# Dilated attention into a SiLU MLP on one core: transposes and products of a kind in one clump each, loads of later batches issued in the second layer

## The chip, the core and the metric

The kernel runs on one core of a Trainium2 chip. The metric is device time in microseconds (us) of one execution; less is better. Times of several executions are given as their median with the lowest and highest. A core has five engines with instruction queues of their own that run side by side and wait for each other by semaphores: TensorE (PE in the profile: matmuls, with PEld for its weight loads), VectorE (DVE), ScalarE (ACT), GpSimd (POOL, here almost only the issue of loads) and SyncE (SP, the issue of stores). Each engine takes its own instructions in order.

## The reference

Inputs are q, k and v of 8 batches, 8 heads, 576 positions and 64 channels, and two matrices, w_in (512x2048) and w_out (2048x512).

```python
scores = q @ k.T / 8                     # per batch and head, 576 x 576
rel = row - column
mask = (rel >= 0) & (rel < 32)                              # heads 0 to 3, "plain"
mask = (rel >= 0) & (rel < 128) & (rel % 4 == 0)            # heads 4 to 7, "dilated"
attn = softmax of the scores inside the mask
x = (attn @ v), heads side by side       # 4608 tokens of 512
h = x @ w_in
out = (h * sigmoid(h)) @ w_out           # 4608 x 512, float32
```

Every row looks at 32 positions: of a plain head the last 32, of a dilated head every fourth one of the last 128.

## The kernel before, in words

**Two kinds, blocks of 32 rows.** A batch has two kinds of heads, z=0 (the four plain ones) and z=1 (the four dilated ones). A dilated head is split into 4 residue classes of positions, in each of which it is a plain band. Rows go in blocks of 32 (QB); a block needs 64 keys (KB). So the attention is made of many matmuls that use only a part of TensorE's 128x128 array: 64x64 or 64x32 of it, as the shapes in the profile say. The kernel orders them so that neighbours lie in different quarters of the array.

**The stages of one kind of one batch**, each a function:

- load_qk (L91) and load_v (L124) issue the loads on GpSimd's queue, shift_v (L143) moves rows of v inside the chip. The tiles n0 and n1 (q and k, two buffers each) and vw (v, one for even and one for odd batches) are written.
- transpose (L244): which=1 is k, which=0 is q. 36 small transposes (z=0) or 24 (z=1) on TensorE into two PSUM tiles, which VectorE copies out for one half and ScalarE for the other (L264, L273).
- scores (L392): 72 or 80 small matmuls into three PSUM tiles; VectorE scales and masks them (L414, L423) and takes the row maximum (L430).
- exps (L445): on ScalarE, one exponential of 128x64 for each of 8 or 10 blocks (L458), for hi=0 and hi=1, the two heads of a pair.
- normal (L463): on VectorE, the reciprocal of the row sum and its product with the exponentials, pn (L471 to L474).
- turn and turned (L478, L487): 4 or 5 full-array transposes of pn on TensorE (L483), copied out by VectorE (L491).
- values (L493): the products with v, 32 small matmuls for each of two *phases* (L519) and 4 or 8 more for the last 64 rows (last_values, L565 and L576). A PSUM tile belongs to one pair of heads, n. In phase 0 the even blocks of n=0 and the odd blocks of n=1 are done, in phase 1 the others, so that the two row halves of the array never write the same bank at one time.
- finish (L589): after each phase VectorE copies the halves just made into xT (L598, and L585 or L587 for the last rows).

**The MLP.** layer1 (L602) multiplies xT of one batch by one of 16 column tiles f of w_in: 8 full-array matmuls (L607) into a PSUM tile h of the pool big, then Silu on ScalarE (L615). layer2 (L635) makes 4 (even batches) or 5 (odd ones) output tiles of 128 tokens, 16 matmuls each (L643), copied out by VectorE (L651) and stored by SyncE's queue (L653). Batch 0 has its first layer in two parts (L619).

**PSUM.** It has 8 banks. The pool big has 2 buffers of two banks, shared by h and o; the pool ps has 4 buffers of one bank for all else.

**The order by hand.** The order of the instructions is the order in which the program issues them (a manual schedule). Each batch has a plan (plan_of, L676) that hangs attention work of the next batches between its matmuls. A plan has *steps*: step f (0 to 15) is just ahead of the column tile f of the first layer, step 16 + 4x + y just ahead of the y-th four matmuls of output tile x. at(s, fn, ...) appends a call to step s. The helpers transposes (L659) and later (L663) spread the work of one kind over steps; later's six steps are: normal of hi=0, turn of hi=0, normal of hi=1, turn of hi=1, products of phase 0, products of phase 1. For batches b from 2 on (L732 to L749) the plan holds, in the first layer, the transposes of z=1 and the whole later part of z=0 of batch b+1, then the scores of z=1; in the second layer the transposes and scores of z=0 of batch b+2 and the later part of z=1 of batch b+1.

A step only fixes the place in each engine's queue. An instruction starts when its engine reaches it and the semaphores that it waits for are set. The table of ScalarE's functions (Exp or Silu) has to be changed twice a batch (ACT_TABLE_LOAD); the build puts such a load ahead of the first activation that needs it. A copy needs none.

The plan is called from layer2's loop (L642) and from the outer loop (L801):

```python
                if f % 4 == 0:
                    plan(NFF + 4 * x + f // 4)
...
            for f in range(NFF):
                plan(f)
                layer1(b, f)
        layer2(b, plan)
```

Of the kernel before, what the change touches and what calls it, by code (L numbers as in the profile page):

```python
# [14 lines left out]
P = 128  # L15
W = 32
DIL = 4
# [10 lines left out]
def kernel(  # L28
# [461 lines left out]
        pt = a["pt", z, hi] = ptp.tile([P, WM // 2, P], F16, tag="pt", name=f"ptT_{b}_{z}_{hi}")  # L490
        nc.vector.tensor_copy(pt[:, 0:n], a["ptT", z, hi][:, 0:n])  # L491

    def values(b, z, phase):  # L493

        a = att(b)
        if phase == 0:
            a["x", z] = [
                ps.tile([P, NS], F32, tag="ps", name=f"x_{b}_{2 * z + n}") for n in (0, 1)
            ]
            a["xs", z] = ps.tile([P, 2, KB], F32, tag="ps", name=f"xs_{b}_{z}")  # L500

        for i in range(8):
            for n in (0, 1):
                e = (n + phase) % 2
                r = slice(e * KB, e * KB + KB)
                for hi in (0, 1):
                    x = a["x", z][n][hi * D : hi * D + D]
                    pt = a["pt", z, hi]
                    if z == 0:
                        j = 2 * i + e  # L510
                        w = plain_v(a, j, 2 * n + hi)
                        dst = x[:, j * QB : (j + 1) * QB]
                        p = pt[r, 2 * n + j // 8, i % 4 * QB : i % 4 * QB + QB]
                    else:
                        j, c = i // 4 * 2 + e, i % 4
                        w = class_v(a, j, 2 * n + hi, c)
                        dst = x.rearrange("d (i r) -> d r i", r=DIL)[:, c, j * QB : (j + 1) * QB]
                        p = pt[r, 2 * n + j // 2, c * QB : c * QB + QB]
                    nc.tensor.matmul(dst, w, p, start=True, stop=True)  # L519
        last_values(b, z, phase)  # L520

    def values0(z, part):


        a = att(0)
        x = a["x", z] = [
            ps.tile([P, 2, SA], F32, tag="ps", name=f"x_0_{z}_{part}_{e}") for e in (0, 1)
        ]
        pt = a["pt", z, part]
        for i in range(4):  # L530
            for n in (0, 1):
                for e in (0, 1):
                    for hi in (0, 1):
                        dst = x[e][hi * D : hi * D + D, n]
                        if z == 0:
                            j = 8 * part + 2 * i + e
                            w = plain_v(a, j, 2 * n + hi)
                            dst = dst[:, (2 * i + e) * QB : (2 * i + e + 1) * QB]
                        else:
                            w = class_v(a, 2 * part + e, 2 * n + hi, i)  # L540
                            dst = dst.rearrange("d (i r) -> d r i", r=DIL)[:, i, e * QB : e * QB + QB]
                        nc.tensor.matmul(
                            dst, w, pt[e * KB : e * KB + KB, 2 * hi + n, i * QB : i * QB + QB],
                            start=True, stop=True,
                        )
        if part:
            a["xs", z] = ps.tile([P, 2, KB], F32, tag="ps", name=f"xs_0_{z}")
            last_values(0, z, 0)

    def finish0(z, part, copy=nc.vector.tensor_copy):  # L550
# [5 lines left out]
        if part:  # L556
            last_finish(0, z, 0, copy)

    def last_values(b, z, phase):
        a = att(b)  # L560
        r = slice(phase * KB, phase * KB + KB)
        for hi in (0, 1):
            if z == 0:
                for n in (0, 1):
                    nc.tensor.matmul(  # L565
                        a["xs", z][hi * D : hi * D + D, n, phase * QB : (phase + 1) * QB],
                        plain_v(a, 16 + phase, 2 * n + hi),
                        a["pt", z, 1][r, 4, (2 * n + hi) * QB : (2 * n + hi + 1) * QB],
                        start=True, stop=True,
                    )  # L570
            else:
                x = a["xs", z][hi * D : hi * D + D, phase].rearrange("d (i r) -> d r i", r=DIL)
                for c in range(DIL):
                    o = (2 * hi + c % 2) * QB
                    pt = a["pt", z, 1][r, 4 + c // 2] if b == 0 else a["pt", z, c // 2][r, 4]
                    nc.tensor.matmul(  # L576
                        x[:, c, :], class_v(a, 4, 2 * phase + hi, c), pt[:, o : o + TL],
                        start=True, stop=True,
                    )

    def last_finish(b, z, phase, copy=nc.vector.tensor_copy):
        xT, xs = att(b)["xT"], att(b)["xs", z]
        if z == 0:
            o = phase * QB
            copy(xT[:, 0:2, NS + o : NS + o + QB], xs[:, :, o : o + QB])  # L585
        else:
            copy(xT[:, 2 + phase, NS:S], xs[:, phase])  # L587

    def finish(b, z, phase, copy=nc.vector.tensor_copy):  # L589


        a = att(b)
        xT = a["xT"]
        run = QB * (DIL if z else 1)
        for n in (0, 1):
            e = (n + phase) % 2
            f = lambda y: y.rearrange("d (m e c) -> d m e c", e=2, c=run)[:, :, e, :]
            copy(f(xT[:, 2 * z + n, 0:NS]), f(a["x", z][n]))  # L598
        last_finish(b, z, phase, copy)


    def layer1(b, f):  # L602
# [53 lines left out]

    both = (nc.vector.tensor_copy, nc.scalar.copy)

    def transposes(at, b, z, steps):  # L659
        for n in (0, 1):  # L660
            at(steps[n], transpose, b, z, 1 - n, both)

    def later(at, b, z, steps):  # L663

        at(steps[0], normal, b, z, 0)
        at(steps[1], turn, b, z, 0)
        at(steps[1], turned, b, z, 0)
        at(steps[2], normal, b, z, 1)
        at(steps[3], turn, b, z, 1)
        at(steps[3], turned, b, z, 1)  # L670
        at(steps[4], values, b, z, 0)
        at(steps[4], finish, b, z, 0)
        at(steps[5], values, b, z, 1)
        at(steps[5], finish, b, z, 1)

    def plan_of(b):  # L676
        ev = {}
# [8 lines left out]
        if b == 0:  # L686

            at(-15, normal, 0, 1, 1)
            at(-14, turn, 0, 1, 1)
            at(-14, turned, 0, 1, 1)  # L690
            at(-13, normal, 0, 0, 1)
            at(-12, values0, 1, 1)
            at(-12, finish0, 1, 1)
            at(-10, turn, 0, 0, 1)
            at(-10, turned, 0, 0, 1)
            at(-8, last_values, 0, 1, 1)
            at(-8, last_finish, 0, 1, 1)
            at(-7, values0, 0, 1)
            at(-7, finish0, 0, 1)
            at(-3, last_values, 0, 0, 1)  # L700
            at(-3, last_finish, 0, 0, 1)
            transposes(at, 1, 0, (1, 3))
            at(5, scores, 1, 0)
            transposes(at, 1, 1, (7, 9))
            at(10, load_qk, 3)
            at(10, load_v, 2)
            at(10, shift_v, 2, nc.gpsimd, (ALL,))
            at(12, scores, 1, 1)
            for hi in (0, 1):
                at(12, shift, 1, 1, hi)  # L710
            at(14, shift_v, 1, nc.sync, (ALL,))
            all_exps(1, 0)
            all_exps(1, 1)
            later(at, 1, 0, (20, 22, 23, 25, 26, 27))
            later(at, 1, 1, (25, 27, 27, 29, 30, 31))
        elif b == 1:
            at(0, load_v, 3)
            at(0, shift_v, 3, nc.gpsimd, (ALL,))
            transposes(at, 2, 0, (2, 4))
            transposes(at, 2, 1, (8, 10))  # L720
            transposes(at, 3, 0, (14, 15))
            at(6, scores, 2, 0)
            at(11, load_qk, 4)
            at(12, scores, 2, 1)
            all_exps(2, 0)
            all_exps(2, 1)
            at(17, scores, 3, 0)
            at(18, exps, 3, 0, 0)
            at(18, exps, 3, 0, 1)
            later(at, 2, 0, (22, 24, 25, 27, 28, 29))  # L730
            later(at, 2, 1, (29, 31, 32, 34, 35, 36))
        else:  # L732
            if b + 2 < B:
                at(0, load_v, b + 2)
                at(0, shift_v, b + 2, nc.gpsimd, (ALL,))
            if b + 1 < B:
                transposes(at, b + 1, 1, (2, 6))
                later(at, b + 1, 0, (0, 2, 2, 4, 7, 8))
                if b + 3 < B:
                    at(8, load_qk, b + 3)  # L740
            if b + 2 < B:
                transposes(at, b + 2, 0, (12, 14))
                at(17, scores, b + 2, 0)
                at(18, exps, b + 2, 0, 0)
                at(18, exps, b + 2, 0, 1)
            if b + 1 < B:
                at(10, scores, b + 1, 1)
                all_exps(b + 1, 1)
                later(at, b + 1, 1, (22, 24, 25, 27, 28, 29))  # L749

        def plan(s):
            for fn, args in ev.pop(s, ()):
# [84 lines left out]
```

## Time and profile before

| what | us |
|---|---|
| three runs: median (lowest to highest) | 348.04 (346.62 to 348.13) |
| the profiled execution | 348.62 |
| its span, first to last instruction | 346.8 |
| TensorE busy | 321.5 (93%) |
| ScalarE busy | 216.4 (62%) |
| VectorE busy | 184.6 (53%) |
| GpSimd busy | 88.3 (25%) |

The profile is that of one execution. "Busy" of TensorE counts matmuls from start to modelled end, and they overlap; distances between the starts of neighbouring groups say more. A line of a timeline reads: start, busy time, engine, line of the program, operation, written tile <- read tiles, shape, count, and in brackets idle time ahead of it and what ended it. In rows of stretches PEclk is the clock granted to TensorE, 1.00 being full. The costliest groups are the second layer's matmuls (L643, 132.2), the first layer's (L607, 119.1), the exponentials (L458, 94.2) and Silu (L615, 72.8).

### The profile page before, as it was taken

The numbers are of one execution on the slowest core, as the hardware profiler recorded it, in microseconds if no ns is written. First come the engines' busy times: TensorE is split into PE (matmuls) and PEld (weight loads), VectorE is DVE, ScalarE is ACT, GpSimd is POOL, SyncE is SP. The second block draws the span as 40 slices with busy tenths as digits, with TensorE's granted clock in tenths as the row PEclk, the third lists the DMA queues.
The fourth block names the chain that finished last, engine by engine and source line by source line (L and its number), as shares of the span: only waits on it lengthen the run. The fifth ranks groups of instructions, "written<-read, shape, count | busy, mean of one in ns | idle before, by whom it ended". The sixth has DMA issues, their size and how long they took to land.

```text
span 346.8 us, 11988 instructions
## 1 busy us (share of the span) xinstructions
PE 321.5 (93%) x5216; PEld 203.4 (59%) x5216; DVE 184.6 (53%) x410; ACT 216.4 (62%) x746; POOL 88.3 (25%) x148
## 2 busy tenths in 40 slices
PE   4549899889999999999999999999999999999995
PEld 4437654447754577557765577557755577457642
DVE  7766337765657756555656356555656353440021
ACT  2693547506699756995589365995589356916400
POOL 8726656333400254024400560023000000000000
PEclk9999989999999999999999999999999999999999
DMA  6999999939802199029901964039002100110022
GB/s 81 164 219 208 205 200 219 187 75 136 132 10 93 60 131 144 33 66 144 150 8 66 174 110 75 33 81 145 4 2 92 62 4 2 60 50 14 0 79 76
DMA packets 45062, 32.90 MB, mean 95 GB/s; under 512 B 21872, under 2 KB 39536, under 8 KB 45008
## 3 DMA queue, kind: packets, MB, share of 16 engines
q0 software_dynamic: 38816, 21.74, 45.8%
q1 hardware_dynamic: 6192, 10.39, 8.5%
q8 instruction: 41, 0.67, 0.8%
q14 instruction: 13, 0.11, 0.1%
HBM read 37.75 MB, written 9.44 MB: 136 GB/s over the span
## 4 chain that ended last, share of the span: by engine, by line
PE 76%; DVE 8%; DMA 6%; ACT 5%; issue 2%; POOL 1%; SPq 0%; POOLq 0%
PE h L607 30%; PE o L643 27%; PE h L626 6%; ACT pe L458 4%; PE t L260 3%; PE x L519 3%; DVE pn L474 3%; PE pt L483 2%; DMA vw<-in_v_dram 2%; DMA vw<-vw 2%; DMA n<-in_k_dram 2%; ACT L458 1%; PE s L318 1%; DVE kC L273 1%; PE s L306 1%
## 5 line engine op out<-in xcount | busy, mean ns | idle before, releaser
L643 PE MATMUL o<-w_out,gT 128*128 128x512 f16 x576 | 132.2, 379 | 0.0
L615 ACT ACTIVATE gT<-h 128x576 f16<-128x576 f32 x112 | 72.8, 650 | 84.0 <-PE h L607 84.0
L607 PE MATMUL h<-xT,w_in 128*128 128x288 f16 x896 | 119.1, 286 | 0.0
L607 PEld LDWEIGHTS <-w_in 128*128 128x128 f16 x896 | 84.2, 98 | 22.6 <-issue 0.2
L458 ACT ACTIVATE pe<-ms,nm 128x64 f32<-128x64 f32 x284 | 94.2, 333 | 3.3 <-DVE nm L387 3.2
L643 PEld LDWEIGHTS <-gT 128*128 128x128 f16 x576 | 53.8, 98 | 58.0
L651 DVE COPY ob<-o 128x512 f32<-128x512 f32 x36 | 24.8, 690 | 59.1 <-PE o L643 59.1
L458 ACT ACTIVATION_READ_ACCUMULATOR pe<-ms,nm 128x1 f32 x284 | 53.0, 187 | 0.0
L414 DVE SCALAR_TENSOR_TENSOR ms<-s,mask 128x512 f32<-128x512 f32 x28 | 19.2, 687 | 33.1 <-PE ss L306 15.3
L127 POOL DMA_DIRECT2D vw<-in_v_dram x16 | 10.0, 632 | 98.1 <-PE xs L576 98.1
L598 DVE CAST xT<-x 128x256 f16<-128x256 f32 x56 | 21.1, 418 | 11.5 <-PE xs L565 7.4
L474 DVE TENSOR_TENSOR pn<-pe,r 128x640 f16<-128x640 f32 (+2 forms) x32 | 25.3, 792 | 1.1
L430 DVE TENSOR_REDUCE nm<-ms 128x10 f32<-128x640 f32 (+1 forms) x28 | 22.0, 787 | 1.0
L626 PE MATMUL h<-xT,w_in 128*128 128x256 f16 (+1 forms) x128 | 20.6, 317 | 0.8 <-DVE xT L555 0.8
L491 DVE COPY ptT<-pt 128x640 f16<-128x640 f16 (+2 forms) x32 | 15.0, 470 | 11.4 <-PE pt L483 11.4
L633 ACT ACTIVATE gT<-h 128x512 f16<-128x512 f32 (+1 forms) x16 | 10.4, 650 | 16.3 <-PE h L626 16.3
L102 POOL DMA_DIRECT2D n<-in_q_dram x28 | 16.3, 592 | 15.5 <-DMA w_in<-in_moe_w_in_dram 5.5
L483 PE MATMUL pt<-ident,pn 128*128 128x128 f16 x152 | 14.7, 229 | 5.6 <-DVE pn L474 5.2
L102 POOL DMA_DIRECT2D n<-in_k_dram x28 | 16.3, 591 | 10.4 <-DMA w_in<-in_moe_w_in_dram 3.6
L483 PEld LDWEIGHTS <-pn 128*128 128x128 f16 x152 | 10.0, 101 | 13.7 <-DVE pn L474 11.1
L519 PEld LDWEIGHTS <-vw 64*64 64x64 f16 x896 | 9.8, 108 | 10.9 <-issue 10.9
L626 PEld LDWEIGHTS <-w_in 128*128 128x128 f16 x128 | 12.9, 107 | 5.1 <-issue 0.8
(79 smaller groups left out, 260.2 us busy)
## 6 DMA issues: line engine op xcount, KB each, us to landing
out_dram<-ob SPq DMA_DIRECT2D x36, 256.0 KB, 2.0
n<-in_k_dram POOLq DMA_DIRECT2D x28, 144.0 KB, 5.3
n<-in_q_dram POOLq DMA_DIRECT2D x28, 144.0 KB, 5.3
vw<-in_v_dram POOLq DMA_DIRECT2D x8, 288.0 KB, 6.1
vw<-in_v_dram POOLq DMA_DIRECT2D x16, 128.0 KB, 3.3
w_in<-in_moe_w_in_dram POOLq DMA_DIRECT2D x4, 512.0 KB, 10.7
w_out<-in_moe_w_out_dram POOLq DMA_DIRECT2D x4, 512.0 KB, 10.6
vw<-vw POOLq DMA_DIRECT2D x12, 128.0 KB, 3.8
```

Of the source, the lines that this page charges most:

```text
L102: nc.gpsimd.dma_start(out=qk[b, z, which][i * HF : i * HF + UPS[z]].rearrange("p h u d -> p h (u d)"), in_=src[b, h : h + 2].rearrange("h ...
L430: nc.vector.tensor_reduce(out=nm[:, 0:w], in_=ms[:, 0:w], axis=AX.X, op=ALU.max, negate=True)
L458: nc.scalar.activation(pe[:, t, :], ms[:, t, :], AF.Exp, bias=nm[:, t : t + 1], accum_out=l[:, t : t + 1],)
L474: nc.vector.tensor_tensor(pn[:, 0:w], a["pe", z, hi][:, 0:w], r[:, 0:w, None].broadcast_to([P, w, KB]), ALU.mult)
L483: nc.tensor.transpose(t[:, i, :], a["pn", z, hi][:, 2 * i : 2 * i + 2].rearrange("p t c -> p (t c)"), ident)
L519: nc.tensor.matmul(dst, w, p, start=True, stop=True)
L598: copy(f(xT[:, 2 * z + n, 0:NS]), f(a["x", z][n]))
L607: nc.tensor.matmul(h[:, half, 0:HS], w_in16[:, c, f * P : f * P + P], xT[:, c, half * HS : half * HS + HS], start=(c == 0), stop=(c == MC ...
L615: nc.scalar.activation(gT[:, f, s0 : s0 + S].rearrange("p (a c) -> p a c", a=2), h[:, :, 0:HS], AF.Silu)
L626: nc.tensor.matmul(h[:, i, 0 : c1 - c0], w_in16[:, c, (f + i) * P : (f + i + 1) * P], xT[:, c, c0:c1], start=(c == 0), stop=(c == MC - 1),)
L643: nc.tensor.matmul(o, gT[:, f, t * P : (t + 1) * P], w_out16[:, f, :], start=(f == 0), stop=(f == NFF - 1),)
L651: nc.vector.tensor_copy(ob, o)
```

## The change

Four things are done.

1. transposes takes one step: k and q of a kind are transposed one right after the other. For batches from 2 on those of z=1 go from steps 2 and 6 to step 0.
2. values has no phases any more. All 64 products of a kind, and then the last rows, are issued in one clump, into two PSUM tiles that belong each to a row half e of the array instead of a pair of heads; the last rows have a tile for each half too. finish copies each tile whole.
3. later has four steps in place of six: normal of hi=0, normal of hi=1, both turns, all products.
4. In the plans of the batches from 1 on, load_v and load_qk are called at steps 16 and 17 in place of 0, 8 and 11.

The number of matmuls and their shapes are as before, and so is each load.

```diff
-    def values(b, z, phase):
+    def values(b, z):
         a = att(b)
-        if phase == 0:
-            a["x", z] = [
-                ps.tile([P, NS], F32, tag="ps", name=f"x_{b}_{2 * z + n}") for n in (0, 1)
-            ]
-            a["xs", z] = ps.tile([P, 2, KB], F32, tag="ps", name=f"xs_{b}_{z}")
+        x = a["x", z] = [
+            ps.tile([P, 2, SA], F32, tag="ps", name=f"x_{b}_{z}_{e}") for e in (0, 1)
+        ]
         for i in range(8):
             for n in (0, 1):
-                e = (n + phase) % 2
-                r = slice(e * KB, e * KB + KB)
-                for hi in (0, 1):
...
+                for e in (0, 1):
+                    r = slice(e * KB, e * KB + KB)
+                    for hi in (0, 1):
+                        dst = x[e][hi * D : hi * D + D, n]
...
+                        nc.tensor.matmul(dst, w, p, start=True, stop=True)
+        a["xs", z] = [
+            ps.tile([P, 2, QB], F32, tag="ps", name=f"xs_{b}_{z}_{e}") for e in (0, 1)
+        ]
+        for e in (0, 1):
+            last_values(b, z, e)
...
+    def finish(b, z, copy=nc.vector.tensor_copy):
+        a = att(b)
         run = QB * (DIL if z else 1)
...
+        for e in (0, 1):
+            copy(
+                a["xT"][:, 2 * z : 2 * z + 2, 0:NS].rearrange("d n (m e c) -> d n m e c", e=2, c=run)[:, :, :, e, :],
+                a["x", z][e].rearrange("d n (m c) -> d n m c", c=run),
+            )
+        for e in (0, 1):
+            last_finish(b, z, e, copy)
...
-    def transposes(at, b, z, steps):
-        for n in (0, 1):
-            at(steps[n], transpose, b, z, 1 - n, both)
+    def transposes(at, b, z, step):
+        for which in (1, 0):
+            at(step, transpose, b, z, which, both)
 
     def later(at, b, z, steps):
...
+        for hi in (0, 1):
+            at(steps[hi], normal, b, z, hi)
+        for fn in (turn, turned):
+            for hi in (0, 1):
+                at(steps[2], fn, b, z, hi)
+        at(steps[3], values, b, z)
+        at(steps[3], finish, b, z)
...
-            transposes(at, 1, 0, (1, 3))
+            transposes(at, 1, 0, 1)
             at(5, scores, 1, 0)
-            transposes(at, 1, 1, (7, 9))
+            transposes(at, 1, 1, 8)
...
-            later(at, 1, 0, (20, 22, 23, 25, 26, 27))
-            later(at, 1, 1, (25, 27, 27, 29, 30, 31))
+            later(at, 1, 0, (20, 22, 25, 26))
+            later(at, 1, 1, (25, 27, 29, 30))
         elif b == 1:
-            at(0, load_v, 3)
-            at(0, shift_v, 3, nc.gpsimd, (ALL,))
-            transposes(at, 2, 0, (2, 4))
-            transposes(at, 2, 1, (8, 10))
-            transposes(at, 3, 0, (14, 15))
+            at(16, load_v, 3)
+            at(16, shift_v, 3, nc.gpsimd, (ALL,))
+            transposes(at, 2, 0, 2)
+            transposes(at, 2, 1, 9)
+            transposes(at, 3, 0, 15)
             at(6, scores, 2, 0)
-            at(11, load_qk, 4)
+            at(17, load_qk, 4)
...
-            later(at, 2, 0, (22, 24, 25, 27, 28, 29))
-            later(at, 2, 1, (29, 31, 32, 34, 35, 36))
+            later(at, 2, 0, (22, 24, 27, 28))
+            later(at, 2, 1, (29, 31, 33, 34))
         else:
             if b + 2 < B:
-                at(0, load_v, b + 2)
-                at(0, shift_v, b + 2, nc.gpsimd, (ALL,))
+                at(16, load_v, b + 2)
+                at(16, shift_v, b + 2, nc.gpsimd, (ALL,))
             if b + 1 < B:
-                transposes(at, b + 1, 1, (2, 6))
-                later(at, b + 1, 0, (0, 2, 2, 4, 7, 8))
+                transposes(at, b + 1, 1, 0)
+                later(at, b + 1, 0, (0, 0, 4, 6))
                 if b + 3 < B:
-                    at(8, load_qk, b + 3)
+                    at(16, load_qk, b + 3)
             if b + 2 < B:
-                transposes(at, b + 2, 0, (12, 14))
+                transposes(at, b + 2, 0, 13)
                 at(17, scores, b + 2, 0)
...
             if b + 1 < B:
-                at(10, scores, b + 1, 1)
+                at(9, scores, b + 1, 1)
                 all_exps(b + 1, 1)
-                later(at, b + 1, 1, (22, 24, 25, 27, 28, 29))
+                later(at, b + 1, 1, (22, 24, 27, 28))
```

## The prediction

> **What bounds the kernel now.** I read the page first (parts 1 and 4), then TensorE's timeline of one steady batch, then ScalarE's, then the early batches. All times are us.
>
> ```profile
> PE 321.5 (93%) x5216; PEld 203.4 (59%) x5216; DVE 184.6 (53%) x410; ACT 216.4 (62%) x746; POOL 88.3 (25%) x148
> ...
> PE 76%; DVE 8%; DMA 6%; ACT 5%; issue 2%; POOL 1%; SPq 0%; POOLq 0%
> ```
>
> TensorE is the bound: busy 93% of the span, and 76% of the chain that ended last. The full-array matmuls (L607, L643) are not touched, so the change can move only what stands between them: the clumps of small matmuls, and TensorE's waits.
>
> ```profile
> 210.59 2.13 PE L607 MATMUL h<-xT,w_in 128*128 128x288 f16 x16
> 212.65 0.48 PE L260 MATMUL t<-ident,n 64*64 64x64 f16 x36
> 213.06 2.13 PE L607 MATMUL h<-xT,w_in 128*128 128x288 f16 x16
> ...
> 228.40 1.03 PE L643 MATMUL o<-w_out,gT 128*128 128x512 f16 x4
> 229.36 0.45 PE L519 MATMUL x<-ptT,vw 64*64 64x32 f16 x32
> 229.63 0.30 PE L576 MATMUL xs<-ptT,vw 64*64 64x16 f16 x8
> 229.86 1.04 PE L643 MATMUL o<-w_out,gT 128*128 128x512 f16 x4
> ```
>
> This is TensorE's timeline in batch 4: start, busy, group. Read the distances between starts. Undisturbed, 128 h matmuls take 15.68 (chain, at 310.08), 0.1225 each, and 80 o matmuls 17.28, 0.216 each. Here 16 h need 1.96, but with the 36 transposes the next 16 start 2.47 later: the clump costs 0.51. Its 36 weight loads span 0.37, of which the last takes 0.10, so they start 7.7 ns apart and 36 take 0.28. The other **0.23 is a fixed price of a clump**, whatever is in it. For the products: from 228.40 to 229.86 is 1.46, less 4 o (0.86), 0.60; 32 cost 0.25 and the 8 of xs about 0.15, fixed 0.20. So a merge of two clumps saves 0.20 to 0.23; I take 0.21. The lowest reading is 0.10, the entry alone (229.36 - 228.40 - 0.86).
>
> **What the merges save.** In the instruction order of the two builds TensorE has the same 5216 matmuls, in 76 small clumps before and 48 after: 14 merges of transposes and 14 of products. Of the turns (L483) two sets of five become one of ten; they are full-array work, 5 cost 0.28 (225.25 to 225.53), and joining them saves 0.02 each time. The waits ahead of them matter more: a turn now comes later, after both normals.
>
> - Batch 0, first layer: two merges, but one stands ahead of a 2.06 gap at 41.97 that no instruction of the program releases ("issue"); arriving sooner only lengthens that. 0.3.
> - Batch 0, second layer: walked below, 0.5.
> - Batch 1, first layer: 3 merges, 0.6.
> - Batch 1, second layer: 2 merges, 0.4, and three waits for VectorE's pn:
>
> ```profile
> 98.02 6.22 PE L643 MATMUL o<-w_out,gT 128*128 128x512 f16 x28
> 104.73 0.40 PE L483 MATMUL pt<-ident,pn 128*128 128x128 f16 x4 [0.49 <-DVE pn L474]
> ```
>
> 28 o take 6.05, so the turn was due at 104.07 and came 0.66 late; those at 112.89 and 116.19 are late by 0.46 and 0.42. After the change the first turn stands behind 44 o, at 96.34 + 9.5 + 0.83 (scores) = 106.7, and the second at about 113.2 (0.50 + 0.86 + 0.83 + 20 o). ScalarE's exponentials go on as before (pitch 0.332 from 98.50): the second half of each kind ends at 104.5 and 111.1, its pn 1.4 later. Both are in time: 1.5 saved. What is late next is the copy of the turned tile, which ends within 0.1 of the products' turn. The next batch's first 16 h (2.40 at 119.42, elsewhere 2.12) wait for the last half of xT; now transposes stand there: 0.3. Together 2.2.
> - Batches 2 to 5: four merges, 0.84, and the second turn's wait of 0.25 (due at 199.71 + 1.96 = 201.67, came at 201.92): 1.1 each, 4.4.
> - Batch 6: three merges, 0.63, the same 0.25, and waits of 0.50 in its second layer (turns at 300.5 and 303.4): 1.4.
>
> Sum: 0.3 + 0.5 + 0.6 + 2.2 + 4.4 + 1.4 = **9.4 saved**. At 0.10 a merge it would be 6.5.
>
> **What is added: the table load.** For batches 2 to 6 the transposes of z=1 move from steps 2 and 6 to step 0, ahead of the first h. Each issues a ScalarE copy (L273), and ScalarE works in order. In the changed build's order the load of the Silu table, placed ahead of the first Silu, now stands *behind* the two copies.
>
> ```profile
> 218.38 1.28 ACT L458 ACT_TABLE_LOAD   x1
> 219.67 0.35 ACT L458 ACTIVATE pe<-ms,nm 128x64 f32<-128x64 f32 x1
> ...
> 232.39 1.28 ACT L615 ACT_TABLE_LOAD   x1
> ...
> 233.95 2.12 PE L607 MATMUL h<-xT,w_in 128*128 128x288 f16 x16
> ...
> 235.13 0.65 ACT L615 ACTIVATE gT<-h 128x576 f16<-128x576 f32 x1 [1.46 <-PE h L607]
> ...
> 236.01 0.47 PE L260 MATMUL t<-ident,n 48*128 48x48 f16 x24
> ...
> 236.66 0.63 ACT L273 COPY kC<-t 128x576 f16<-128x576 f16 x1
> ```
>
> Before, the load at 232.39 follows the last exponential and is over before the layer begins. After, count from the first transpose: k copy at 0.65 (236.66 - 236.01), q copy 0.55 later (the pitch at which a copy follows a Silu at 77.95 and 78.50), done at 1.83, load 1.85 to 3.13, first Silu to 3.79. TensorE: 48 transposes to 0.71 (24 take 0.41, 24 more 0.30), two h groups to 2.68. The third h needs the first one's buffer (pool big has two), free at 3.79 + 0.05: **a wait of 1.16**, five times, 5.8. Queued behind that third h is all of TensorE. Between 0.9 and 1.5 each, for the copies' pitch and the release: 4.5 to 7.5. VectorE's two normals, now both here, end near 4.7, and the turn is due at 5.8: covered.
>
> The Trainium skill, "ScalarE: Activation LUTs", What ACT_TABLE_LOAD costs, gives 1283 ns for the load and another 1380 ns of drain for every switch. The row agrees on the first and not on the second: the first exponential starts 1.29 after the load does. By the page the five waits would be 2.5 each, and the change a loss of about 5.
>
> **Batch 0, second layer.** pn of the second half ends at 64.02 there, since ScalarE sets it:
>
> ```profile
> 64.07 0.45 PE L483 MATMUL pt<-ident,pn 128*128 128x128 f16 x5 [0.64 <-DVE pn L474]
> ...
> 71.65 0.45 PE L483 MATMUL pt<-ident,pn 128*128 128x128 f16 x5 [1.27 <-DVE pn L474]
> ```
>
> The first turns now follow 36 o, at 61.9, and wait till 64.07: one wait of 1.9 for two of 0.9 and 0.6, and from 64.36 both builds stand alike. Then 4 o, products (0.83), 12 o to 68.7, while VectorE does two turned copies, row sum, pn, the four copies of finish and the second chain: pn at 71.24. TensorE is idle for 2.3, and the rest (ten turns, 4 o, products, 8 o) ends at 75.3 against 75.79: 0.5 saved.
>
> But long idling costs the clock:
>
> ```profile
> 43.00:44.00 1.00, 0.00 (x0) 0.00 (x0) 0.46 (x1) 0.00 (x0) 0.48 (x1) 1.00 1.27 201
> ...
> 45.00:46.00 1.00, 1.00 (x6) 0.46 (x3) 0.96 (x2) 0.00 (x0) 0.00 (x0) 0.50 1.64 183
> ```
>
> After the 2.06 gap the granted clock (the third column from the right) is 0.50 for about 3.4, in which 320-column matmuls come every 0.267 in place of 0.134: 1.7 lost. After the 1.27 wait before 71.65 it stays 1.00. So 1.16 at a layer's start should be safe, and 2.3 is likely not: I charge 1.5, between 0 and 3.4 (two such drops). "TensorE: Matmul & The Clock Gate", Part 1, says in the Trainium skill that the clock falls after an idle window of about 3.4; by it neither wait would cost anything, and the sum would be 1.5 lower. This trace shows the drop after 2.06.
>
> **At nothing.** The loads: on GpSimd's queue they stand in the same order in both builds and wait for the same kinds of instruction (last products of the buffer's batch, last transposes of the n tile), not for a step, so a later step delays none. q's may start some 3 earlier, since its transposes do. No steady transpose waits for a DMA, which is the cover; without it a load costs 5.3 (median to landing). SP's stores keep their order. VectorE has 28 casts fewer, off the path: two of 128x256 (0.76 together) become one of 128x512, unseen; between 0.6 and 0.8 by the 0.69 of ob and those 0.76. The four PSUM buffers that a clump now takes at once come from copies that end over 0.5 earlier, but for 0.1 in the first two batches.
>
> **The sum.** -9.4 + 5.8 + 1.5 = -2.1. The profiled execution took 348.62 (span 346.8 and 1.8 around); that makes 346.5 there. It stands 0.58 above the median, 348.04, so the forecast is **345.9**, -0.6%. 0.5% (1.74) is about what a measurement of this kernel can tell from no change.
>
> **Rivals.**
> - *The first table load is hidden anyway*: the wait at the layer's start is gone, -9.4 + 1.5 = -7.9, 340. For it: ScalarE idles over 1 ahead of the layer. Against: in-order execution behind copies that need the new transposes.
> - *Merging pays little*: 0.10 a merge, -6.5 + 5.8 + 1.5 = +0.8, 348.8. For it: only the entry is seen as a gap. Against: clumps of unlike size fit one fixed price of 0.2.
> - *The clock falls at every layer's start* (the side of slower): five drops of 1.7, +8.5 - 2.1 = +6.4, 354.5; from two drops on the change does not gain. The place is the third h of batches 2 to 6, and what decides is how much idling a window of 3.4 bears: between 1.27 and 2.06. For it: 1.16 is close. Against: 1.27 did not do it.
> - *The change doesn't do what it says*: so with the loads, as said; worth 0, inside the forecast.
>
> **Chances.** Forecast (344 to 347.5) 0.55, hidden load 0.10, small merges 0.20, clock or longer table waits 0.15. The range 342 to 351 takes in the first and third case, the bounds of the waits (4.5 and 7.5) and drops (0 and 3.4), and leaves out most of the hidden load and of the repeated drop. Faster by over 0.5% (under 346.3): 0.10, and of the forecast's 0.55 some 0.43: 0.53; slower (over 349.8): 0.15 and some of the third case, 0.19; the rest 0.28.
>
> **What would show it.** Right: 48 small clumps, of 72 transposes at about 0.79 and products at 0.83 and 1.0; a table load right behind two L273 copies in batches 2 to 6, and the third h some 1.2 late; no late turn in batches 1 to 6; POOL in its old order. Wrong: a table load that starts before the copies, clumps that cost the sum of their parts, or a clock below 1 at the layers' starts.

## The result, and the profile after

The changed kernel takes **344.00 us** (median of four runs, 343.49 to 344.45) against 347.52 of the kernel before (four runs, 346.62 to 348.13): a ratio of 0.990, 95% interval 0.9868 to 0.9932. It is faster by 1.0%. The forecast was 345.9, faster by 0.6%, in a range of 342 to 351.

The profiled execution took 343.56, with a span of 341.8 (before: 348.62 and 346.8). The page of the changed kernel, its parts 1, 4 and one line of part 5 (busy, mean ns of one | idle time just before, and what ended it):

```profile
PE 314.5 (92%) x5216; PEld 204.4 (60%) x5216; DVE 180.5 (53%) x382; ACT 216.6 (63%) x746; POOL 88.3 (26%) x148
...
PE 78%; ACT 9%; DMA 5%; DVE 3%; issue 2%; POOL 1%; SPq 0%; POOLq 0%
...
L610 PE MATMUL h<-xT,w_in 128*128 128x288 f16 x896 | 115.9, 287 | 4.5 <-ACT gT L618 4.5
```

TensorE has the same 5216 matmuls in 7.0 less busy time, and VectorE 28 instructions fewer. ScalarE's share of the chain that ended last went from 5% to 9%, and h, which had no idle time ahead of it before (L607, 0.0), now waits 4.5 for Silu (L618; L615 before). Both sides of the forecast are there: cheaper clumps, and a wait that the change added.

TensorE's timeline of the changed kernel around the end of batch 4 (start, busy, group), the place shown of the kernel before:

```profile
223.20 0.72 PE L483 MATMUL pt<-ident,pn 128*128 128x128 f16 x10
223.76 1.03 PE L646 MATMUL o<-w_out,gT 128*128 128x512 f16 x4
224.72 0.71 PE L516 MATMUL x<-ptT,vw 64*64 64x32 f16 x64
225.25 0.39 PE L581 MATMUL xs<-ptT,vw 64*64 64x16 f16 x16
225.58 3.63 PE L646 MATMUL o<-w_out,gT 128*128 128x512 f16 x16
229.14 0.77 PE L260 MATMUL t<-ident,n 48*128 48x48 f16 x48
```

From 223.76 to 225.58 is 1.82; less four o (0.864) the products cost 0.95 to 0.96. Before, the first of the two clumps cost 0.60 (228.40 to 229.86, shown in the prediction), and the second, from 229.86 to 231.35 less four o, 0.63:

```profile
230.83 0.48 PE L519 MATMUL x<-ptT,vw 64*64 64x32 f16 x32
231.12 0.30 PE L576 MATMUL xs<-ptT,vw 64*64 64x16 f16 x8
231.35 2.76 PE L643 MATMUL o<-w_out,gT 128*128 128x512 f16 x12
```

The transposes now stand in front of the next layer. What that does to ScalarE shows in the trace of the changed kernel a moment later, both engines together:

```profile
229.68 0.64 ACT L273 COPY kC<-t 128x576 f16<-128x576 f16 x1 [1.94 <-PE t L260]
229.84 2.13 PE L610 MATMUL h<-xT,w_in 128*128 128x288 f16 x16
230.21 0.65 ACT L273 COPY qC<-t 128x576 f16<-128x576 f16 x1
230.88 1.28 ACT L618 ACT_TABLE_LOAD   x1
232.17 1.19 ACT L618 ACTIVATE gT<-h 128x576 f16<-128x576 f32 x2
232.87 0.53 PE L610 MATMUL h<-xT,w_in 128*128 128x288 f16 x3 [0.90 <-ACT gT L618]
```

ScalarE idles for 1.94, long enough for the table load of 1.28, but two copies that need the new transposes stand ahead of it. The load starts at 230.88, the first Silu after it, and the third h (17th matmul) starts at 232.87. By distances, 16 h from 229.84 should have ended the wait at 231.80: it is 1.06 late, the same in batches 2 to 6.

Where the time went, from the traces (us; a batch counts from its first h to the next batch's; the 0.80 of the transposes that moved ahead of the first h is put to the batch whose plan issues them):

| stretch | before | change forecast | change measured |
|---|---|---|---|
| start to the first h | 26.96 | 0 | -1.19 |
| batch 0, first layer | 27.27 | -0.3 | +0.32 |
| batch 0, second layer | 21.55 | +1.0 | -0.80 |
| batch 1 | 43.62 | -2.5 | -2.68 |
| batch 2 | 37.21 | -0.24 | -0.37 |
| batches 3 to 5 | 117.72 | +0.18 | -0.30 |
| batch 6 | 35.57 | -0.24 | +0.04 |
| batch 7 | 36.85 | 0 | 0.0 |
| sum | | -2.1 | -4.98 |

The program is the same in both kernels up to the first h. Over all traces of this study that start lies between 25.5 and 28.0, so its -1.19 is chance, and the change itself is worth -3.8 in the traces, -3.5 in the medians.

### The profile page after: what moved, and what is told of

Same layout as the page of the kernel before. It is cut to its first block, busy times and chain, and to the rows that moved or that the text cites. A ratio compares the mean times of both kernels' runs of the same rounds, so it can differ in the third digit from the quotient of the medians.

```text
span 341.8 us, 11965 instructions
## 1 busy us (share of the span) xinstructions
PE 314.5 (92%) x5216; PEld 204.4 (60%) x5216; DVE 180.5 (53%) x382; ACT 216.6 (63%) x746; POOL 88.3 (26%) x148
## 4 chain that ended last, share of the span: by engine, by line
PE 78%; ACT 9%; DMA 5%; DVE 3%; issue 2%; POOL 1%; SPq 0%; POOLq 0%
PE o L646 31%; PE h L610 30%; PE h L629 6%; ACT pe L458 4%; PE t L260 3%; PE x L516 2%; PE pt L483 2%; DMA vw<-in_v_dram 2%; ACT L618 2%; DMA vw<-vw 2%; DMA n<-in_k_dram 2%; PE s L306 1%; PE s L318 1%; DVE pn L474 1%; ACT gT L618 1%
## 5 line engine op out<-in xcount | busy, mean ns | idle before, releaser
L646 PE MATMUL o<-w_out,gT 128*128 128x512 f16 x576 | 129.5, 380 | 0.0
L610 PE MATMUL h<-xT,w_in 128*128 128x288 f16 x896 | 115.9, 287 | 4.5 <-ACT gT L618 4.5
L618 ACT ACTIVATE gT<-h 128x576 f16<-128x576 f32 x112 | 72.3, 650 | 64.3 <-PE h L610 63.5
L610 PEld LDWEIGHTS <-w_in 128*128 128x128 f16 x896 | 85.3, 98 | 27.5 <-issue 5.4
L646 PEld LDWEIGHTS <-gT 128*128 128x128 f16 x576 | 54.7, 98 | 61.7
L597 DVE CAST xT<-x 128x512 f16<-128x512 f32 x28 | 18.0, 685 | 12.0 <-PE xs L570 10.3
L491 DVE COPY ptT<-pt 128x640 f16<-128x640 f16 (+2 forms) x32 | 13.9, 469 | 13.8 <-PE pt L483 13.6
L483 PE MATMUL pt<-ident,pn 128*128 128x128 f16 x152 | 12.7, 228 | 4.7 <-DVE pn L474 4.7
L629 PEld LDWEIGHTS <-w_in 128*128 128x128 f16 x128 | 13.2, 108 | 5.5 <-issue 0.8
L273 ACT COPY kC<-t 128x576 f16<-128x576 f16 x7 | 4.5, 637 | 15.4 <-PE t L260 15.4
```

Source lines behind the costliest of these rows:

```text
L483: nc.tensor.transpose(t[:, i, :], a["pn", z, hi][:, 2 * i : 2 * i + 2].rearrange("p t c -> p (t c)"), ident)
L597: copy(a["xT"][:, 2 * z : 2 * z + 2, 0:NS].rearrange("d n (m e c) -> d n m e c", e=2, c=run)[:, :, :, e, :], a["x", z][e].rearrange("d n ( ...
L610: nc.tensor.matmul(h[:, half, 0:HS], w_in16[:, c, f * P : f * P + P], xT[:, c, half * HS : half * HS + HS], start=(c == 0), stop=(c == MC ...
L618: nc.scalar.activation(gT[:, f, s0 : s0 + S].rearrange("p (a c) -> p a c", a=2), h[:, :, 0:HS], AF.Silu)
L629: nc.tensor.matmul(h[:, i, 0 : c1 - c0], w_in16[:, c, (f + i) * P : (f + i + 1) * P], xT[:, c, c0:c1], start=(c == 0), stop=(c == MC - 1),)
L646: nc.tensor.matmul(o, gT[:, f, t * P : (t + 1) * P], w_out16[:, f, :], start=(f == 0), stop=(f == NFF - 1),)
```

## The experiments

**My theory**: the clumps have a fixed price, the late turns of batch 1 are gone, and from both is taken a Silu table load that waits behind two copies. **Rivals**: the moved loads made the gain; the table load's wait costs nothing, or stands for something else at step 0; a clump costs only what it holds; the late turns only change place; the clock decides. In the comparisons below medians are set against 344.00 (the changed kernel) or 338.45 (the step-2 kernel), and each ratio is to the kernel before, measured beside it. One part of the diff has no experiment of its own: from batch 2 on the scores of z=1 are issued at step 9 in place of 10. Their 80 matmuls take 0.85 in both traces (209.74 to 210.59 before, 204.29 to 205.14 after).

**1. Transposes at step 2.**

```diff
-                transposes(at, b + 1, 1, 0)
+                transposes(at, b + 1, 1, 2)
```

> The changed kernel with one number altered: the transposes of z=1 of batches 3 to 7 are issued at step 2 of the first layer in place of step 0, still in one clump. My theory: the load of the Silu table then stands ahead of the two ScalarE copies again, runs while the second layer ends, and the wait of the third h (1.06 in each of batches 2 to 6 in the trace of the changed kernel) is gone: 5.3 less, 344.0 - 5.3 = 338.7, and no idle time of TensorE at the layers' starts. Rival, the wait is only passed on (ScalarE's two copies of 0.53 then hold up the Silu of the third h, or the later turn): 343 to 345. Rival, the clock: if idling of 1.06 at a layer's start also cost some clock, the gain is above 5.3.

Measured: 338.45 (337.56 to 339.22), ratio 0.9719 (0.9693 to 0.9744): 5.6 less than the changed kernel. In the trace each of the five layers is 1.06 shorter, 5.3 in all. Both engines at the start of batch 5's first layer:

```profile
224.58 1.28 ACT L618 ACT_TABLE_LOAD   x1
224.78 1.24 PE L646 MATMUL o<-w_out,gT 128*128 128x512 f16 x5
225.85 2.12 PE L610 MATMUL h<-xT,w_in 128*128 128x288 f16 x16
227.03 0.65 ACT L618 ACTIVATE gT<-h 128x576 f16<-128x576 f32 x1 [1.17 <-PE h L610]
```

The load now lies beside the end of the second layer, and ScalarE even waits 1.17 for the first h. Nothing else grew: the wait was not passed on. This is the fastest kernel of the study, 2.8% below the kernel before.

**2. The loads back at their old steps** (load_v at 0, load_qk at 8 and 11, all else as changed).

> The changed kernel with its loads back at the old steps (load_v and its shift at step 0, load_qk at steps 8 and 11); all else as changed. My theory: a step does not delay or hasten a load, which waits for the buffer's last reader, so 0: 344.0, within 0.5. Rival, the gain of the change came from the loads that were moved away from the first layer: 3.5 more, back at 347.5.

Measured: 344.43 (342.74 to 345.27), ratio 0.9882 (0.9853 to 0.9912). From batch 1 on every layer agrees with the changed kernel within 0.02. The fourth part of the change does nothing to the time.

**3. Transposes split again**, on the step-2 kernel.

```diff
-            at(step, transpose, b, z, which, both)
+            at(step + 1 - which, transpose, b, z, which, both)
...
-            transposes(at, 3, 0, 15)
+            transposes(at, 3, 0, 14)
```

> The step-2 kernel with k and q of a kind transposed in two clumps again, q one step after k, for all 14 kinds (of batch 3's z=0 at steps 14 and 15). To be compared with the step-2 kernel. My theory: a clump has a fixed price, 0.15 (z=0, 7 of them) and 0.20 (z=1, 7) by the two traces: 14 more clumps are 2.4 more, between 2.0 and 2.8. Rival, merging pays little (0.10 a clump): 1.4 more. Rival, a clump costs only what it holds: 0.

Measured: 340.76 (339.60 to 342.44), ratio 0.9793 (0.9765 to 0.9821): 2.3 more. TensorE at the start of batch 5's first layer:

```profile
226.52 2.12 PE L610 MATMUL h<-xT,w_in 128*128 128x288 f16 x16
228.57 0.47 PE L260 MATMUL t<-ident,n 48*128 48x48 f16 x24
228.98 1.15 PE L610 MATMUL h<-xT,w_in 128*128 128x288 f16 x8
230.06 0.47 PE L260 MATMUL t<-ident,n 48*128 48x48 f16 x24
230.47 1.15 PE L610 MATMUL h<-xT,w_in 128*128 128x288 f16 x8
```

From 226.52 to 228.98 is 2.46, less 16 h (1.96) 0.50; the second half costs 0.51. So every half costs 0.50 to 0.51 again, where 48 in one clump cost 0.80 and 72 cost 0.86: 0.21 and 0.16 a merge, 0.37 in each steady batch.

**4. Products in two halves**, in batches 3 to 7, on the changed kernel.

```diff
-        for i in range(8):
+        for i in (range(8), range(4), range(4, 8))[0 if part is None else 1 + part]:
...
+        at(steps[3], values, b, z, 0)
+        at(steps[3] + 1, values, b, z, 1)
+        at(steps[3] + 1, finish, b, z)
```

> The changed kernel with the products of batches 3 to 7 issued in two halves, the second one step (2 h or 4 o tile matmuls' worth) after the first; the PSUM tiles and the copies stay as changed, and the copies follow the second half. 10 more clumps. To be compared with the changed kernel. My theory: 0.23 (z=0) and 0.27 (z=1) each by the traces, 2.5 more, 346.5. Rival, merging pays little (0.10 a clump): 1.0 more. Rival, what counted was the bank per row half and not the merge: 0.

Measured: 345.60 (344.60 to 347.33), ratio 0.9936 (0.9912 to 0.9959): 1.6 more, less than expected and more than the rival. Its trace tells the price more closely (TensorE, second layer of batch 4):

```profile
226.41 1.03 PE L650 MATMUL o<-w_out,gT 128*128 128x512 f16 x4
227.37 0.45 PE L518 MATMUL x<-ptT,vw 64*64 64x32 f16 x32
227.75 1.04 PE L650 MATMUL o<-w_out,gT 128*128 128x512 f16 x4
228.71 0.45 PE L518 MATMUL x<-ptT,vw 64*64 64x32 f16 x32
228.99 0.36 PE L585 MATMUL xs<-ptT,vw 64*64 64x16 f16 x16
229.28 2.76 PE L650 MATMUL o<-w_out,gT 128*128 128x512 f16 x12
```

From 227.75 to 229.28 is 1.53, less 0.86: 0.67. The first half, from 226.41 to 227.75 less 0.86, costs 0.47. Together 1.14 against 0.95 in one: 0.19 for the split, and 0.19 to 0.22 in each of the ten layers that have one, 2.0 in all. By distances the products of a kind cost 0.28 (z=1) and 0.25 (z=0) less in the changed kernel than in the one before. Some 0.2 of that is the merge. The other 0.05 to 0.09 goes with the rest of the new layout, since two halves in it cost 1.14 and 1.00 and the two phases before 1.23 and 1.05; whether the order, the banks or the place of the last rows does it is not shown.

**5. Table load pulled ahead, transposes left at step 0.**

```diff
+    def early():
+        nc.scalar.activation(warm[:, 1:2], warm[:, 0:1], AF.Silu)
...
+                at(0, early)
                 transposes(at, b + 1, 1, 0)
```

> The changed kernel with its transposes still at step 0, but in batches 2 to 6 ScalarE gets a Silu of one column of a zeroed tile ahead of the two copies, whose result nobody reads. My theory: it is only the place of the table load in ScalarE's order that costs; now the load starts when the last exponential has ended (ScalarE then idles for 1.94 in batch 5 of the changed kernel's trace, the load takes 1.28), and the third h comes without a wait: 5.3 less than the changed kernel, the same time as the step-2 kernel, within 0.5. Rival, it is the transposes at step 0 themselves that cost (copies ahead of the first Silu, two normals behind VectorE's copies): no gain, or less than half of it.

Measured: 339.47 (338.65 to 340.88), ratio 0.9770 (0.9738 to 0.9802): 4.5 less than the changed kernel. In the trace each of the five layers is 1.06 shorter, as with step 2, 5.3 in all. Batches 0 and 1, whose plans the edit leaves alone, have second layers that are 0.48 and 0.33 longer in this execution (for batch 0 see the clock below).

```profile
225.46 1.28 ACT L665 ACT_TABLE_LOAD   x1
...
226.75 0.20 ACT L665 ACTIVATE warm<-warm 128x1 f32<-128x1 f32 x1
...
227.38 0.64 ACT L273 COPY kC<-t 128x576 f16<-128x576 f16 x1 [0.42 <-PE t L260]
227.54 3.73 PE L610 MATMUL h<-xT,w_in 128*128 128x288 f16 x29
```

The copies stand where they stood in the changed kernel, and 29 h follow without a wait. So it is the place of the load in ScalarE's order that costs, and not the transposes at step 0. The Trainium skill ("ScalarE: Activation LUTs", What ACT_TABLE_LOAD costs) adds 1380 ns of drain to each load; here the Silu starts 1.29 after the load's start (225.46 to 226.75), as in the other traces.

**6. Rising waits.** The second q copy of step 0 is repeated 1, 2, 3, 4 and 5 times in batches 2 to 6.

> The changed kernel with ScalarE's second q copy of step 0 repeated once in batch 2, twice in batch 3, and so on to five times in batch 6 (the same data to the same place). So the third h's wait, 1.06 before, should be 1.59, 2.12, 2.65, 3.18 and 3.71, by 0.53 a copy: 8.0 more in all. It asks from which wait on the granted clock falls after it. My prediction's rival put that between 1.27 and 2.06, so that four of the five layers would lose 1.7 more each: 14.8 more than the changed kernel. If the clock bears them all: 8.0 more, and 1.00 in all rows of stretches from 115 on. If the threshold lies at 3 or above, one or two layers lose 1.7 or so.

Measured: 357.53, one run. A repeated copy takes 0.67, not 0.53, so the third h waits 1.73, 2.40, 3.07, 3.74 and 4.41. The layers grew by 0.67, 1.34, 3.68, 4.35 and 4.72: the first two by the copies alone, the others by 1.67, 1.67 and 1.37 more, with a granted clock of 0.50 for 3.41 after the wait. My expected threshold, between 1.27 and 2.06, is wrong: here 2.40 cost no clock. But in the kernel before a gap of 2.06 did, so the length of a wait can't be the rule.

**7. Each turn right behind its normal**, on the step-2 kernel, in all batches from 1 on.

> The step-2 kernel with the turn of each half issued as early as before the change, right behind the normal of its half (five steps in later in place of four); transposes and products stay merged. To be compared with the step-2 kernel. My theory: the turns in batch 1's second layer are late again for pn (0.66, 0.46 and 0.42 before the change), 1.5 more; nothing in batches 2 to 5, since the normal of the second half keeps its place ahead of the copies here; in batch 0's second layer one long wait becomes two short ones, within 0.5 either way: 1.5 more in all, between 1.0 and 2.0. Rival, the late turns only move a wait that the products would have had anyway (for the turned copies): 0.

Measured: 342.57 (341.71 to 344.08), ratio 0.9858 (0.9831 to 0.9885): 4.1 more, well over the 1.5. The test was not clean. Batch 1's second layer grew by 2.2 (late turns of 0.66, 0.24 and 1.28; the last one stood a step earlier than before the change), and batch 2's first turn came 0.78 late. In batches 2 to 6 the transposes stood right behind a turn, and the two together cost 1.33 where apart they cost 0.23 and 0.80; why is open.

**8. The same in batch 2's kinds alone**, at the old steps.

```diff
-            later(at, 2, 0, (22, 24, 27, 28))
-            later(at, 2, 1, (29, 31, 33, 34))
+            later(at, 2, 0, (22, 24, 25, 27, 28))
+            later(at, 2, 1, (29, 31, 32, 34, 35))
```

> The step-2 kernel with only the plan of batch 1 changed back in one respect: the later part of both kinds of batch 2 has five steps, each turn right behind the normal of its half, at the steps of the kernel before (22, 24, 25, 27 and 29, 31, 32, 34), with the products merged at 28 and 35. It leaves out what disturbed the run before (transposes right behind a turn). To be compared with the step-2 kernel. My theory: the late turns are worth what the trace of before showed, 0.66 + 0.46 + 0.42 = 1.5, and the products one step later hold up batch 2's first h by 0.3: 1.8 more, between 1.2 and 2.3, all of it between the starts of batch 1's second layer and batch 2's second layer. Rival, the waits only change their place: 0 to 0.5.

Measured: 339.67 (338.74 to 340.62), ratio 0.9784 (0.9754 to 0.9813): 1.2 more by the medians; by the ratios, each to its own runs of the kernel before, the distance is 0.0065, 2.3. The trace tells it more closely: batch 1's second layer is 1.34 longer and batch 2's first 0.27, 1.61 in all; every other layer from batch 1 on agrees within 0.02. By distances the late turns are 0.66, 0.24 and 0.42; two of them as TensorE's timeline has them:

```profile
101.39 0.40 PE L483 MATMUL pt<-ident,pn 128*128 128x128 f16 x4 [0.49 <-DVE pn L474]
...
112.28 0.45 PE L483 MATMUL pt<-ident,pn 128*128 128x128 f16 x5 [0.25 <-DVE pn L474]
```

So the late turns were a real loss, and when the change moved them back nothing later took their place.

**9. Five equal waits of 2.40** (two repeated copies in each of batches 2 to 6).

> The changed kernel with the second q copy of step 0 repeated twice in each of batches 2 to 6: the third h waits 2.40 in each (1.06 + 2 x 0.67), 6.7 more than the changed kernel in all by the copies alone. Theory from the runs so far: the granted clock is set anew every 3.413, and is 0.50 for one such window after a window in which TensorE was busy less than some 0.46 of the time (idle over 1.84); so a wait of 2.40 costs clock only where 1.84 of it falls into one window. The windows stand still against the program's start by chance, so about three of the five layers should lose 1.7 more each, the others nothing, and the trace should show which by its windows' busy shares, with none between on the wrong side of 0.46. Rival, a wait itself has a threshold between 2.40 (no drop in the run with rising waits) and 3.07 (a drop): none of the five drops. Rival, any idling over 2 costs clock: all five.

Measured: 352.54, one run. All five waits are 2.40, and four layers grew by 1.34, the copies alone. Batch 4's grew by 3.00. One dropped, not three; which one agrees with the theory. Stretches laid on the grid of 3.413 that the clock's own changes give (TensorE's busy time is the second number; the clock the third column from the right), around the waits of batches 2 and 4:

```profile
116.58:119.99 3.41, 2.01 (x16) 1.47 (x15) 3.27 (x8) 3.33 (x5) 1.81 (x3) 1.00 1.19 165
119.99:123.41 3.42, 2.58 (x27) 2.16 (x26) 0.33 (x2) 2.39 (x5) 0.08 (x1) 1.00 1.08 115
...
198.50:201.91 3.41, 1.25 (x11) 1.00 (x11) 1.37 (x4) 2.69 (x5) 3.41 (x7) 1.00 0.89 162
201.91:205.33 3.42, 3.42 (x22) 2.49 (x20) 0.91 (x2) 1.22 (x2) 1.56 (x3) 0.50 1.08 163
```

Batch 2's wait straddles an edge: 2.01 and 2.58 busy, and the clock stays. Batch 4's lies within one window, 1.25 busy (0.37), and the next window has 0.50.

## Why the prediction was right, and where it was not

The side and the mechanism hold; the sum was 1.7 short of the traces without the start, and 344.00 is the lower edge of the forecast's own band (344 to 347.5). By its own steps:

- **The price of a merge** (0.21, from 0.10 to 0.23): right in the mean. Read from the traces of the two kernels it is 0.16 and 0.20 for transposes and, with what else the new layout does, 0.25 and 0.28 for products, 0.22 in the mean; so it is not one price whatever the clump holds. Experiments 3 and 4 confirm it by undoing: 0.16 and 0.21, and some 0.2. The Trainium skill ("TensorEngine Tiling (Array Packing)", Key Properties) says that a change of the tiling mode drains TensorE; it gives no price. Each clump is entered and left once, which fits, but no run here separates the drain from other costs of entry. Clumps of 72 transposes cost 0.86, not 0.79; those of products 0.80 and 0.95, not 0.83 and 1.0.
- **The table load's wait** (1.16, five times): right in place and cause (experiments 1 and 5), a little large: 1.06. The k copy starts 0.54 after the first transpose, not 0.65. This is 0.5 of the 1.7. By an estimate with the 1380 ns of drain that the Trainium skill ("ScalarE: Activation LUTs", What ACT_TABLE_LOAD costs) adds, each wait would have been 2.4; the traces show no such drain.
- **Batch 1** (2.8 with batch 2's first h): right, -2.68 and part of batch 2's. Experiment 8 measures the late turns and that first h at 1.61, for 1.5 + 0.3.
- **Batches 2 to 5** (1.1 each without the table load): right. Batch 4 takes 36.94 before (20.49 and 16.45 for its two layers) and 35.79 in the step-2 kernel (19.62 and 16.17), 1.15 less, and no turn waits there any more.
- **Batch 0, second layer**: the walk without clock was nearly right. The two waits are 1.7 and 2.0 (forecast 1.9 and 2.3), and the layer ends 0.80 sooner (0.5). **The charge of 1.5 for the clock is the step that failed.** It was put on by the length of the wait, and the clock goes by the busy share of a fixed window. Here it hangs on little, and is cheaper when it strikes; rows of the changed kernel and of experiment 5 in this layer:

```profile
67.56:70.97 3.41, 1.59 (x16) 0.85 (x13) 3.31 (x9) 0.00 (x0) 1.07 (x2) 1.00 0.44 96
```

```profile
61.67:65.08 3.41, 1.38 (x15) 0.73 (x19) 3.27 (x7) 2.57 (x4) 1.10 (x2) 1.00 1.57 168
65.08:68.50 3.42, 3.42 (x78) 1.85 (x77) 3.32 (x9) 0.00 (x0) 1.71 (x4) 0.50 1.00 172
```

  The changed kernel's window around the wait of 2.0 has 1.59 busy, 0.47, and is followed by full clock; experiment 5's, around the first wait, has 1.38, 0.40, and is followed by 0.50. Of nine traces with this layer's new order, three (experiments 4, 5 and 9) dropped there. In all three one small VectorE instruction ahead of the turns (L471 of 128x10; L473 in experiment 9), 0.17 in the changed kernel, took 0.79 to 0.88, and the first wait was 2.3 to 2.4 in place of 1.7; what held it is open. The layer then took 21.2 to 21.4, where the others took 20.6 to 20.75. The price of 1.7 was that of a layer where TensorE sets the pace; here the second turn waits for VectorE, and its wait shrank from 2.0 to under 0.5.
- **Batch 6**: the waits of 0.50 were to go, and did not; the layer's ten turns come 0.50 late. There are no scores in that layer, so 44 o bring TensorE to the turns at 298.62, while the last exponential ends at 297.9 and its pn at 299.3. A turn that is moved back is on time only if the work that it is moved past is long enough, and I did not walk this layer. 0.3 missed.
- **Batch 0, first layer**: forecast -0.3, found +0.32. In all traces that layer takes 26.6 to 28.2, with its gap of 2.0 to 2.8 and one drop of the clock, whatever the kernel, and it begins at half clock for a time that varies (last section); nothing about the change can be read from it.
- **The loads at nothing**: right (experiment 2). VectorE's new casts take 0.69 (forecast 0.6 to 0.8), off the path.
- **Rivals.** *The load is hidden anyway*: no, undoing it gave 5.3. *Merging pays little*: no, 0.16 to 0.2 a merge by undoing, not 0.10. *The clock falls at every layer's start*: no. With a wait of 1.06 the emptiest window is 0.74 busy; in experiments 6 and 9 a wait that put 1.70 of idling into one window (0.50 busy, batch 6 of experiment 9) cost no clock, and one that put 2.15 there (batch 4, shown above) cost 1.67.

## What to carry to other kernels

Look at what an added instruction puts itself ahead of on its own engine: two harmless copies, in front of an implicit table load, cost 5.3 of the some 9 that the rest of the change had earned, and moving them by two steps gave it back. Small-tile matmuls pay some 0.2 us for each time that the stream goes to them and back, so putting them together is worth as many times 0.2 as clumps vanish, and no more. A moved consumer is late or on time by the end of its producer's chain, so each layer with other filling must be walked by itself.

## What the runs showed of the hardware

- **The clock goes by fixed windows.** Every drop lasts 3.41 and starts on one grid of 3.413. I put that grid over eleven traces. From full clock's first entry (some 30 us) to the end of the matmuls, all 17 windows in which TensorE was busy for 0.46 of the time or less were followed by half clock, six of 0.47 to 0.48 once, and none from 0.50 up. The border is not sharp: of the windows in which the matmuls of a trace end, five of 0.14 to 0.35 were followed by half clock, and one of 0.45 (experiment 3) was not. So the same wait of 2.40 costs 1.67 or nothing, by where it lies, and the same program takes a drop in one execution and not in the next (the mean clock is 0.990 to 1.000 in the six runs of experiment 2). The Trainium skill ("TensorE: Matmul & The Clock Gate", Part 1) has the free-running window of 3413 ns, which these runs confirm. It speaks of an idle window; here one that was over half idle was enough.
- **TensorE begins at half clock.** Until its first entry, at 28.7 to 31.9 us in the eleven traces, the clock's record is empty, and a row of stretches shows 1.00 there. But in all of them the 256-column matmuls of batch 0's first layer start every 0.213 before that entry and every 0.109 after it. Two groups of the kernel before, whose first entry is at 30.7:

```profile
29.26 1.76 PE L626 MATMUL h<-xT,w_in 128*128 128x256 f16 x8
31.46 1.05 PE L626 MATMUL h<-xT,w_in 128*128 128x256 f16 x8
```

  So that layer's first 2.8 (experiment 3, 26.6 in all) to 6.0 (experiment 4, 28.2) run at half clock, by where the grid lies.
- A ScalarE copy that repeats the one before it, from the same tile to the same place, takes 0.67 from start to start (experiment 6), and one of another tile 0.53.
